# A rank table in place of a table of moves sets the order of a kernel of two long convolutions and two MLPs

## The chip, the cores and the metric

The kernel runs on one core of one Trainium2 chip. The metric is the device time of one execution in microseconds; less is better. The median of three runs of the kernel before is 847.91 us (849.39, 845.15 and 847.91). The execution that was profiled took 850.39 us.

## What is computed

A tensor x of 2048 rows of 640 passes four residual steps, twice a gated long convolution and twice a two-layer MLP with ReLU. Cut to what matters:

```
def _A_ref(q, k, v, shift_k, ssm_k, ssm_D):
    k_shift = sum over t of 4 taps of k, weighted by shift_k      # short causal convolution
    kv = k_shift * v
    y = irfft(rfft(kv, 2S) * rfft(ssm_k, 2S))[:S]                 # causal convolution over 2048 rows, by channel
    y = y + kv * ssm_D
    return q * y

def _B_ref(x, w1, w2):                                            # 640 -> 1728 -> 640
    return maximum(x @ w1, 0) @ w2

x = A_q
x = x + _A_ref(layernorm(x), A_k, A_v, A_shift_k, A_ssm_k, A_ssm_D)
x = x + _B_ref(layernorm(x), B_w1, B_w2)
x = x + _A_ref(layernorm(x), A_k, A_v, A_shift_k, A_ssm_k, A_ssm_D)
x = x + _B_ref(layernorm(x), B_w1, B_w2)
```

## The kernel before

**Tiling.** The rows are cut into 8 chunks of 256 (two tiles of 128 rows each), the channels into 5 tiles of 128. The convolution y is the same in both layers, so it is computed once: for each unit of one or two channel tiles, `transform` makes the spectra of kv and of the filter with small fp32 matmuls (`pg`, `pr` and the transpose `pt`), and `products` multiplies spectra of earlier chunks with filter spectra on VectorE (lines 920 and 925, tiles `pacc` and `pd`), then transforms back with fp32 matmuls (`pq`). Spectra that later chunks need go to DRAM (`A`, `G`) and come back as `Ax` and `Gx`.

**The MLP.** `main` is called 20 times. Each call n runs over seven groups j of the hidden width: `mm1` forms `h{n}_{j}` in PSUM (lines 1449 to 1464), ScalarE makes the fp16 high part `hh`, VectorE the low part `hl` (line 1605), and `mm2` multiplies both with w2 into the banks `o` and `oc` (lines 1433 to 1436). Each fp32 product is three fp16 products of high and low parts. The first two chunks go through the MLP in halves of 128 rows: `mm1` then moves 128 columns, and `mm2` moves 512 and then 128 columns by turns. From chunk 2 on `mm1` moves 256 columns. The calls for chunks 6 and 7 use a Strassen-like form (lines 1384 and 1494). The input of `mm1` is transposed by DMA: four transposes per chunk (line 1318) write `xT{chunk}_{layer}_0{x}`, x = 0 for the high and 1 for the low part, one for each tile of 128 rows. The matmuls of line 1449 with x = 0 need both tiles of part 0.

**fp32 matmuls.** Where a unit has two tiles and comes late enough, `mm3` (lines 577 to 579) makes three matmuls of a rounded fp32 format from the parts of its operands; elsewhere (lines 754, 777, 815, 947, 966) plain fp32 is used, which the trace shows as two records for each matmul.

**What sets the order.** Every operation is recorded in `Plan` with its engine, a cost, what it reads and writes, and a priority. `order` then replays the list in modelled time, and each engine takes the ready operation of the lowest priority for which buffers are free. The result is one fixed instruction stream for each engine, and each engine works through its stream in order; SP's stream issues nearly all DMAs, POOL's the accumulating ones. `best` decides the priorities: operations of class `CRIT` (the start) keep theirs, all others get a key. Before, the keys came from `latest`, which goes backward from the end, repeated four times, and were then pushed about by the table `MOVES`: 693 seeded random nudges of some keys by up to 15 us.

Of the kernel before, what the change touches and what calls it, by code (L numbers as in the profile page):

```python
# [21 lines left out]
P = 128  # L22
S = 2048
# [35 lines left out]
MOVES = ((),) * 4 + (  # L59
# [194 lines left out]
class Plan:  # L254
# [64 lines left out]
    def again(self, kept, key):  # L319
        for o, left, prio in kept[0]:  # L320
            o.left, o.ready, o.start = left, 0.0, None
            if prio[0] != CRIT:
                o.prio = (key[o], o.seq)
# [1513 lines left out]
```

## Time and profile before

| what | before |
| --- | --- |
| runs, us | 849.39, 845.15, 847.91 |
| profiled execution, us | 850.39 |
| its span, first to last instruction, us | 848.6 |
| ScalarE busy | 61% of the span |
| GpSimd busy | 5% of the span |
| HBM traffic over the span | 187 GB/s |

The span is what the rows below cover; 1.8 us of the profiled time lie outside it. Times in a timeline are counted from the span's start. A matmul's start is measured and its length modelled, so its cost in a dense stretch is read from one start to the next.

### The profile page before, as it was taken

The page shows a single profiled execution, that of the slowest core. Times are in us where ns is not written, and L with a number is a line of the kernel's source. Part 1 is how long each engine was busy: PE and PEld are TensorE (multiplying, and loading weights), DVE is VectorE, ACT ScalarE, POOL GpSimd, SP SyncE. Part 2 cuts the span into 40 slices and gives each one's busy share as a digit, 9 for nine tenths or more (in the row PEclk, how much of TensorE's full clock was granted, in tenths as well). Part 3 has the DMA queues.
Part 4 walks back from the last instruction along what each step waited for, and adds up shares of the span by engine and source line. Part 5 has one row for each costly group of instructions (what it writes and reads, how often), then busy time and mean ns, then how long its engine had stood idle before and what let it go on. Part 6 is the DMA issues. An engine that isn't in the chain of part 4 may idle for free.

```text
span 848.6 us, 20004 instructions
## 1 busy us (share of the span) xinstructions
PE 836.8 (99%) x7937; PEld 668.0 (79%) x7937; DVE 778.7 (92%) x1404; ACT 518.3 (61%) x1233; POOL 43.8 (5%) x54
## 2 busy tenths in 40 slices
PE   8999999999998999999999999999999999999998
PEld 6987878888877778777787777777777788888886
DVE  6999999999998899999999999999797799988676
ACT  5798588456784576646657375555515386867531
POOL 0000000000001011011010101010100000000000
PEclk9999999999999999999999999999999999999999
DMA  8995868986989889796997959598977466051200
GB/s 296 394 325 201 266 185 257 313 282 177 314 260 264 277 233 285 233 286 180 226 300 210 260 173 225 164 194 250 247 254 245 115 211 151 22 140 26 58 33 32
DMA packets 138000, 181.68 MB, mean 214 GB/s; under 512 B 53809, under 2 KB 95537, under 8 KB 137906
## 3 DMA queue, kind: packets, MB, share of 16 engines
q1 hardware_dynamic: 129586, 169.91, 65.3%
q0 software_dynamic: 8320, 10.49, 8.3%
q8 instruction: 62, 1.02, 0.5%
q14 instruction: 32, 0.26, 0.1%
HBM read 124.59 MB, written 34.08 MB: 187 GB/s over the span
## 4 chain that ended last, share of the span: by engine, by line
PE 70%; DVE 19%; DMA 4%; ACT 3%; issue 2%; SPq 1%; DVEq 0%; POOLq 0%; ACTq 0%
PE h L1461 8%; PE h L1462 8%; PE h L1464 8%; PE o L1434 6%; PE o L1433 6%; PE o L1384 6%; PE o L1436 6%; PE h L1449 3%; DVE pd L920 3%; DVE pacc L925 3%; PE oc L1433 2%; PE oc L1434 2%; PE pg L754 2%; PE h L1451 1%; PE oc L1436 1%
## 5 line engine op out<-in xcount | busy, mean ns | idle before, releaser
L1461 PE MATMUL h<-xT,w 128*128 128x256 f16 (+1 forms) x1030 | 237.1, 250 | 0.7 <-DVE hl L1610 0.4
L1462 PE MATMUL h<-xT,w 128*128 128x256 f16 (+1 forms) x1030 | 237.0, 250 | 0.0
L1464 PE MATMUL h<-xT,w 128*128 128x256 f16 (+1 forms) x1030 | 237.0, 250 | 0.0
L1433 PE MATMUL o<-w,hh 128*128 128x512 f16 x336 | 127.3, 379 | 0.0
L1434 PE MATMUL o<-w,hh 128*128 128x512 f16 x336 | 127.3, 379 | 0.0
L925 DVE TENSOR_TENSOR pacc<-pacc,pd 128x1536 f32<-128x1536 f32 (+1 forms) x75 | 123.3, 1643 | 0.5
L1462 PEld LDWEIGHTS <-w 128*128 128x128 f16 x1130 | 110.6, 98 | 15.9 <-issue 0.9
L1461 PEld LDWEIGHTS <-w 128*128 128x128 f16 x1130 | 110.5, 98 | 14.7
L1464 PEld LDWEIGHTS <-w 128*128 128x128 f16 x1030 | 100.8, 98 | 6.7
L1604 ACT ACTIVATE hh<-h 128x512 f16<-128x512 f32 (+1 forms) x97 | 46.8, 483 | 71.2 <-PE h L1464 40.3
L1433 PEld LDWEIGHTS <-hh 128*128 128x128 f16 x672 | 65.7, 98 | 29.0
L1434 PEld LDWEIGHTS <-hh 128*128 128x128 f16 x672 | 65.8, 98 | 28.2
L920 DVE TENSOR_TENSOR pd<-Ax,Gx 128x768 f32<-128x768 f32 x83 | 78.1, 949 | 6.7 <-DMA Gx<-G 6.6
L1436 PE MATMUL o<-w,hl 128*128 128x512 f16 x208 | 78.8, 379 | 0.0
L1433 PE MATMUL oc<-w,hh 128*128 128x128 f16 x336 | 73.8, 220 | 0.0
L1434 PE MATMUL oc<-w,hh 128*128 128x128 f16 x336 | 73.6, 219 | 0.0
L1436 PEld LDWEIGHTS <-hl 128*128 128x128 f16 x416 | 40.7, 98 | 25.1 <-DVE hl L1605 0.6
L1449 PE MATMUL h<-xT,w 128*128 128x256 f16 (+1 forms) x400 | 57.4, 251 | 2.2 <-DMA xT<-xh 2.2
L651 ACT ACTIVATE tp<-kt,shs 128x256 f32<-128x256 f32 (+1 forms) x78 | 43.6, 575 | 18.9 <-DVE acc L725 17.2
L1436 PE MATMUL oc<-w,hl 128*128 128x128 f16 x208 | 45.6, 219 | 0.4 <-DVE hl L1605 0.4
L920 DVE TENSOR_TENSOR pd<-at,Gx 128x768 f32<-128x768 f32 x46 | 43.0, 950 | 0.7 <-DMA Gx<-G 0.5
L1449 PEld LDWEIGHTS <-w 128*128 128x128 f16 x400 | 36.3, 98 | 7.8 <-issue 2.5
(276 smaller groups left out, 1974.8 us busy)
## 6 DMA issues: line engine op xcount, KB each, us to landing
Ax<-A SPq DMA_DIRECT2D x89, 384.0 KB, 4.2
Gx<-G SPq DMA_DIRECT2D x89, 384.0 KB, 4.3
G<-gt SPq DMA_DIRECT2D x14, 768.0 KB, 5.0
A<-at SPq DMA_DIRECT2D x14, 768.0 KB, 5.7
ws<-in_w SPq DMA_DIRECT2D x28, 320.0 KB, 6.5
y<-Y SPq DMA_DIRECT2D x22, 320.0 KB, 4.7
x<-in_q SPq DMA_DIRECT2D x16, 320.0 KB, 5.7
gs<-in_hF SPq DMA_DIRECT2D x20, 256.0 KB, 4.7
```

Source lines behind the costliest of these rows:

```text
L651: ACT.activation(o[:, i : i + m], kview(i, m, j), AF.Copy, scale=shs[:, t, j : j + 1])
L920: ew(f"mac{j % POOLMOD}", 768, lambda e, x=dst[i], av=av, gv=gv: e.tensor_mul(x.t, av(), gv()), [ax, gx], [dst[i]], pr_)
L925: dve(768 * (hi - lo), lambda lo=lo, hi=hi, pd=pd: DVE.tensor_add(acc[:, lo:hi], acc[:, lo:hi], pd[:, lo:hi]), [*sums[lo:hi], *dst[lo:hi]] ...
L1384: PE.matmul(b[:, c : c + w], x, y[:, z : z + w], start=done[i] == 1, stop=end, skip_group_check=fin)
L1433: PE.matmul(z, hh[:, c], wh[:, d], start=(j == JS[0] and i == 0 and (h == 0 or s == S[0])), stop=False)
L1434: PE.matmul(z, hh[:, c], wl[:, d], start=False, stop=end and tail)
L1436: PE.matmul(z, hl[:, c], wh[:, d], start=False, stop=end)
L1449: PE.matmul(p[:, z], wh, xv(t, x), start=b and x == 0, stop=e and x == 1)
L1461: PE.matmul(p[:, z], wh, xv(t, 0), start=b, stop=False)
L1462: PE.matmul(p[:, z], wh, xv(t, 1), start=False, stop=tail and e)
L1464: PE.matmul(p[:, z], wl, xv(t, 0), start=False, stop=e)
L1604: act(2 * R, lambda pv_=pv_, hh=hh: ACT.activation(hh.t, pv_(), AF.Relu), [src], [hh], URGENT)
```

## The change

`best` no longer computes keys. It decodes a table `RANKS` with one 16-bit number for each recorded operation and takes that number as the priority; `CRIT` operations keep theirs as before. `latest`, `move`, `again` and `MOVES` are gone. `order`, the recorded operations, their costs, the buffers and everything that is computed are as they were. Both programs have the same instructions on every engine: 7818 matmuls, 1149 activations, 510 DMAs on SP and 40 on POOL. Lines below the table are 124 lower in the changed file (577 becomes 453).

```
-MOVES = ((),) * 4 + (
-    (309216, 1, -282, 918, 30), (849944, 1, -295, 905, 30), (690276, 4, 198, 1398, 30), (179395, 8, 53, 113, 100), (409021, 2, 40, 190, 30), (254445, 4, -151, 249, 30),
...
+RANKS = (
+    "5&#zf000311ONp91^@>D2>=QJ3jhoN4ge1T5C9PX695zd6#y0h7yuan8UPyr9RMBx9{?Z#Apj!)Bmf8iB>*P?0{|QVA^;5lDgY<|D*!A2FaR_FF90(DHvl;RJ^(-fEdVh9H~=;PJOD%hLjXqrO#o2<"
...
     def best(self):
-        ...
-        key = self.latest(*self.order())
-        for move in MOVES:
-            if move:
-                self.move(key, *move)
-            else:
-                key = self.latest(*self.again(kept, key))
-        return self.again(kept, key)
...
+        ranks = np.frombuffer(base64.b85decode(RANKS), "<u2").tolist()
+        for o, r in zip(self.ops, ranks, strict=True):
+            if o.prio[0] != CRIT:
+                o.prio = (r, o.seq)
         return self.order()
```

Three places of the two orders follow.

**TensorE, the first transform of chunk 2** (`pr02_0`, in the call n = 3 of `main`). LDWEIGHTS rows load the weights of the fp16 matmul behind them. Before:

```order
L1462 MATMUL h3_1_2310<-xT0_1_11_2198,w0_11_678 128x128
L1464 LDWEIGHTS w0_11_678
L1464 MATMUL h3_1_2310<-xT0_1_10_2190,w0_11_678 128x128
L577 MATMUL pr02_0_2352<-sh2_0_2264,cMh_1206 128x2x128
L578 MATMUL pr02_0_2352<-sl2_0_2286,cMh_1206 128x2x128
L579 MATMUL pr02_0_2352<-sh2_0_2264,cMl_1722 128x2x128
```

And now:

```order
L1310 MATMUL o20_1929<-w1_51_1317,hh2_5_2223 128x512
L1312 LDWEIGHTS hh2_5_2223
L1312 MATMUL o20_1929<-w1_51_1317,hh2_5_2223 128x512
L453 MATMUL pr02_0_2361<-sh2_0_2201,cMh_1226 128x2x128
L454 MATMUL pr02_0_2361<-sl2_0_2298,cMh_1226 128x2x128
L455 MATMUL pr02_0_2361<-sh2_0_2201,cMl_1804 128x2x128
```

The group stood behind a 128-column matmul of `mm1` and now stands behind a 512-column one of `mm2`. Counted over the two orders, groups of fp32 matmuls other than transposes that stand behind a 128-column 16-bit matmul are 33 before (11 of them of lines 577 to 579) and 19 now (1 of them).

**SP, the transposes for the first call of chunk 2** (`xT2_0_00` and `xT2_0_01`, the high and the low part, read by the matmuls of `h8_0`). `Ax` and `Gx` are spectra, `gs` and `kt` are inputs of later units. Before:

```order
L907 DMA Ax4_0_1_0_4642<-A1_0_103 128x768
L1318 DMA_TRANSPOSE xT2_0_00_4673<-xh2_0_00_4619 128x5x128
L1318 DMA_TRANSPOSE xT2_0_01_4678<-xh2_0_00_4619 128x5x128
L1318 DMA_TRANSPOSE xT2_0_00_4673<-xh2_0_01_4671 128x5x128
L670 DMA gs04_1_4716<-in_hF 128x2x256
L670 DMA gs14_1_4728<-in_hF 128x2x256
L1318 DMA_TRANSPOSE xT2_0_01_4678<-xh2_0_01_4671 128x5x128
L907 DMA Gx4_0_3_0_4760<-G2_0_125 128x768
```

And now:

```order
L783 DMA Ax4_0_1_0_4655<-A1_0_103 128x768
L1194 DMA_TRANSPOSE xT2_0_00_4673<-xh2_0_00_4628 128x5x128
L1194 DMA_TRANSPOSE xT2_0_00_4673<-xh2_0_01_4632 128x5x128
L546 DMA gs04_1_4699<-in_hF 128x2x256
L783 DMA Gx4_0_3_0_4719<-G2_0_125 128x768
L1194 DMA_TRANSPOSE xT2_0_01_4734<-xh2_0_00_4628 128x5x128
L1194 DMA_TRANSPOSE xT2_0_01_4734<-xh2_0_01_4632 128x5x128
```

The second transpose of the high part moved from third to second place; the two of the low part now stand behind one load of `gs` and one of `Gx`. On TensorE the first ten matmuls of `h8_0` keep their place in the sum of matmul work; the first that reads the low part came 5.8 us of matmul work behind them and now comes 3.3 us behind them (ten matmuls of `h8_0`, six of `mm2` and twelve of `pr` stand between).

**VectorE, ahead of the low part of the first hidden group of call 6** (`hh6_0`, line 1605; `h6_2` needs its PSUM bank). Before:

```order
L925 TENSOR_TENSOR pacc3_1_3631<-pacc3_1_3631,pd3_1_2_3678 128x1536
L1676 SCALAR_TENSOR_TENSOR x1_1_1147,sp1_0_1_3830<-oc5_3393,winv_118,x1_1_1147 128x128
L782 TENSOR_TENSOR gt3_3_3879<-pg03_3_3834,ob3_3_3872 128x2x2x128
L1605 SCALAR_TENSOR_TENSOR hh6_0_3877<-h6_0_3764,hh6_0_3877 128x256
L783 TENSOR_TENSOR gt3_3_3879<-pg03_3_3834,ob3_3_3872 128x2x2x128
```

And now:

```order
L1552 SCALAR_TENSOR_TENSOR x1_1_1070,sp1_0_1_3823<-o51_3468,winv_118,x1_1_1070 128x512
L796 TENSOR_TENSOR pd3_1_4_3843<-Ax3_1_2_1_3640,Gx3_1_1_1_3724 128x768
L1552 SCALAR_TENSOR_TENSOR x1_1_1070,sp1_0_1_3823<-oc5_3469,winv_118,x1_1_1070 128x128
L601 TENSOR_TENSOR acc4_0_3769<-acc4_0_3769,tp34_0_3836 128x512
L658 TENSOR_TENSOR gt3_3_3892<-pg03_3_3808,ob3_3_3845 128x2x2x128
L1481 SCALAR_TENSOR_TENSOR hh6_0_3888<-h6_0_3825,hh6_0_3888 128x256
```

Over the whole stream two operations more stand ahead of `hh6_0` than before, the multiply `pd3_1_4` and the tap addition `acc4_0`, which both came behind it. TensorE needs it at the same place of its matmul work.

More of the change, by code (lines that the diff above doesn't have):

```diff
@@ L1 @@
+import base64
 import heapq
@@ L294, in best @@
     def best(self):
-        tiles = list({id(t): t for o in self.ops for t in o.tiles}.values())
-        rings = list({id(t.ring): t.ring for t in tiles if t.ring is not None}.values())
-        kept = [(o, o.left, o.prio) for o in self.ops], [(t, t.left) for t in tiles], [(r, r.free, {k: list(v) for k, v in r.lines.items()}) for r in rings]
-        key = self.latest(*self.order())
-        for move in MOVES:
-            if move:
-                self.move(key, *move)
-            else:
-                key = self.latest(*self.again(kept, key))
@@ L305, in best @@
-        return self.again(kept, key)
-    def move(self, key, seed, by, a, b, part):
-        h = np.arange(len(self.ops), dtype=np.uint32) * np.uint32(2654435761) + np.uint32((seed * 40503 + 12345) % 2**32)
-        for shift, mul in ((16, 2246822519), (13, 3266489917)):
-            h = (h ^ (h >> np.uint32(shift))) * np.uint32(mul)
-        h ^= h >> np.uint32(16)
-        g = h * np.uint32(2654435769)
-        g ^= g >> np.uint32(15)
-        for o, x, y in zip(self.ops, h.tolist(), g.tolist()):
-            if a <= key[o] < b and y % 1000 < part:
-                key[o] += by * (x / 2.0**32 * 2.0 - 1.0)
@@ L319, in again @@
[L319 to L323, printed above, removed]
-        for t, left in kept[1]:
-            t.left = left
-        for r, free, lines in kept[2]:
-            r.free, r.lines = free, {k: list(v) for k, v in lines.items()}
-        return self.order()
-    def latest(self, out, end):
-        users = {}
-        for o in out:
-            for t in o.tiles:
-                users.setdefault(t, []).append(o)
-        left, until = {o: len(o.outs) for o in out}, dict.fromkeys(out, end)
-        before = {o: [(d, (0.0 if o.eng == "PE" else PEOUT) if d.eng == "PE" else 0.08 + (o.eng == "PE") * (RPE * LATE(o) + ROOM.get(d.eng, 0.0))) for d in o.deps] for o in out}
-        spare, had = {}, {}
-        for i, o in enumerate(out):
-            for t in o.new:
-                first = t not in had
-                f = spare.setdefault(t.ring, [(-1.0, j, None) for j in range(t.ring.bufs)])
-                if first:
-                    f.sort(key=lambda x: x[:2])
-                    had[t] = f.pop(0)[2]
-                for u in users.get(had[t], ()):
-                    if u is not o and u not in o.deps:
-                        before[o].append((u, 0.0 if u.eng == o.eng == "PE" else PEOUT if u.eng == "PE" else 0.08))
-                        left[u] += 1
-                if first:
-                    f.append((max(u.ready for u in users[t]), i + len(out), t))
-        unit = lambda o: "DMA" if o.nbytes else o.eng
-        open_, cur, latest = {}, {}, {}
-        for o in out:
-            if not left[o]:
-                open_.setdefault(unit(o), []).append(o)
-        while len(latest) < len(out):
-            t, k = max((min(cur.get(k, end), max(until[o] for o in c)), k) for k, c in open_.items() if c)
-            o = max((o for o in open_[k] if until[o] >= t - 1e-9), key=lambda o: (o.start, o.seq))
-            open_[k].remove(o)
-            cur[k] = t - (o.nbytes / RBW if o.nbytes else o.cost)
-            latest[o] = cur[k] - (1.1 + RLAT if o.nbytes else 0.0)
-            for d, lag in before[o]:
-                until[d] = min(until[d], latest[o] - lag)
-                left[d] -= 1
-                if not left[d]:
-                    open_.setdefault(unit(d), []).append(d)
-        for o in out:
-            if o.cls < -3:
-                latest[o] = o.cls * 1e4
-        return latest
```

62 lines of the change are left out of this document (added), and 115 rows, old and new, of the table MOVES.

## The prediction

> **What bounds the kernel now.** I read the first lines of the page, then the waits of TensorE, then busy time in stretches of the span.
>
> ```profile
> span 848.6 us, 20004 instructions
> PE 836.8 (99%) x7937; PEld 668.0 (79%) x7937; DVE 778.7 (92%) x1404; ACT 518.3 (61%) x1233; POOL 43.8 (5%) x54
> ```
>
> TensorE (PE) is busy for 836.8 of 848.6 us, and the change neither adds nor removes a matmul. So only what lies between the matmuls can go: 11.8 us of idle time, and the slots that are longer than they need be. The waits of TensorE, with the engine waited for, the sum in us, how often, and the longest:
>
> ```profile
> PE h L1449 <- DMA xT<-xh: 2.2, 1, 2.2
> PE spin L1693 <- POOL heps L556: 2.0, 1, 2.0
> PE pr L815 <- ACT sh L810: 1.2, 1, 1.2
> PE pt L801 <- ACT gt L757: 0.7, 1, 0.7
> PE h L1461 <- DVE hl L1610: 0.4, 1, 0.4
> PE oc L1436 <- DVE hl L1605: 0.4, 1, 0.4
> PE o L1384 <- DVE gs L1600: 0.3, 1, 0.3
> PE h L1461 <- DVE hh L1605: 0.2, 1, 0.2
> ```
>
> The second to fourth (3.9 us) are the start; the order of the start is untouched, since its operations are of class CRIT. The other five sum to 3.5 us, and that is all the waiting that a new order can take away. The longest of them is one wait for a DMA transpose.
>
> ```profile
> core 0: us, PE busy (x) PEld busy (x) DVE busy (x) ACT busy (x) POOL busy (x), PEclk, DMA share, GB/s
> 100.00:220.00 120.00, 119.79 (x1394) 98.23 (x1393) 117.20 (x212) 77.62 (x197) 0.00 (x0) 1.00 0.81 256
> 320.00:680.00 360.00, 360.00 (x2983) 274.62 (x2981) 340.17 (x487) 195.93 (x465) 31.77 (x30) 1.00 0.83 226
> ```
>
> From 320 to 680 us TensorE never stands still: nothing can be won there, only lost. From 100 to 220 us VectorE (DVE) is busy for 117.20 of 120 us beside a TensorE at 119.79: two engines are full at once, at full granted clock, and whatever one does later the other must cover.
>
> **The change part by part.** It reorders everything by a few microseconds; I cost the fp32 groups, the transposes, and VectorE's work ahead of TensorE's operands.
>
> *fp32 groups.* Here is one group behind a 512-column matmul, and one behind 128-column ones (start, length):
>
> ```profile
> 299.79 0.38 PE L1436 MATMUL o<-w,hl 128*128 128x512 f16 x1
> 299.82 0.47 PE L577 MATMUL pr<-sh,cMh 128*128 128x256 f32 x1
> 300.12 0.28 PE L578 MATMUL pr<-sl,cMh 128*128 128x256 f32 x1
> 300.24 0.28 PE L579 MATMUL pr<-sh,cMl 128*128 128x256 f32 x1
> ```
>
> ```profile
> 131.47 0.22 PE L1462 MATMUL h<-xT,w 128*128 128x128 f16 x1
> 131.53 0.22 PE L1464 MATMUL h<-xT,w 128*128 128x128 f16 x1
> 131.55 0.36 PE L577 MATMUL pr<-sh,cMh 128*128 128x256 f32 x1
> 131.75 0.28 PE L578 MATMUL pr<-sl,cMh 128*128 128x256 f32 x1
> ```
>
> A matmul of the group takes 0.12 us (300.12 to 300.24), a 128-column one 0.055 us on the mean (131.47 to 131.53). Behind 512 columns, 300.12 - 299.79 = 0.33 us, less the group's own 0.12, leaves 0.21 for the 512 columns, which is 512/128 times the short one's slot: the switch is free. Behind 128 columns, 131.75 - 131.53 = 0.22, less 0.12 and 0.055, leaves 0.045: the switch costs some 0.05 us. Weight loads say why:
>
> ```profile
> L1461 PEld LDWEIGHTS <-w 128*128 128x128 f16 x1130 | 110.5, 98 | 14.7
> L577 PEld LDWEIGHTS pr<-sh,cMh 128*128 128x128 f32 x60 | 11.4, 190 | 1.0
> ```
>
> A load takes 190 ns for these weights and 98 ns for fp16, 92 ns more, too long to hide under one 55 ns slot. The 33 dear entries become 19: 14 x 0.05 = 0.7 us less. Bounds: 0 (if something else holds TensorE there anyway) and 14 x 0.092 = 1.3 us.
>
> [...]
>
> All 33 stand in the stretch of the first two chunks, ahead of the wait for the transpose. So these 0.7 us reach the end only if that wait does not eat them.
>
> *The transposes for `h8_0`.* SP's stream, then the pieces:
>
> ```profile
> 255.31 7.25 SPq L1318 DMA_TRANSPOSE xT<-xh  x3
> 262.62 1.13 SPq L670 DMA_DIRECT2D gs<-in_hF  x2
> 263.80 1.35 SPq L1318 DMA_TRANSPOSE xT<-xh  x1
> 265.24 0.54 SPq L907 DMA_DIRECT2D Gx<-G  x1
> ```
>
> ```profile
> L1318 SPq DMA_TRANSPOSE xT<-xh x1: 1581/1581/1581, 255.3 to 255.3; - x1
> L1318 SPq DMA_TRANSPOSE xT<-xh x2: 2607/2736/2865, 257.0 to 259.7; - x2
> DMA to landing us min/median/max: 6.9/7.0/7.0
> DMA to landing us min/median/max: 4.8/4.8/4.8
> 256.98 0.73 ACT L1290 ACTIVATE xh<-xnB 128x640 f16<-128x640 f32 x1
> 264.48 0.22 PE L1464 MATMUL h<-xT,w 128*128 128x128 f16 x1
> 266.88 0.27 PE L1449 MATMUL h<-xT,w 128*128 128x256 f16 x1 [2.19 <-DMA xT<-xh]
> ```
>
> Each transpose holds SP for 1.35 to 2.9 us. The high part's second one is third, issued at 259.7 and landed 7.0 later (266.7), and TensorE, free since 264.5, starts at 266.88. In the new order it is second: its data are ready at 256.98 + 0.73 = 257.7, SP is free from the first at 256.9, so it goes out at 257.7 and lands at 264.7. The wait all but vanishes: 2.2 us. Late next is the low part. Its two transposes follow at 257.7 + 2.9 = 260.6 plus one `gs` load (0.5) and one `Gx` (0.54), so near 261.7; the last is issued 1.4 to 2.6 later, at 263.1 to 264.3, and lands 4.8 to 7.0 after that: 267.9 to 271.3. TensorE now wants it 3.3 us behind 264.7, at 268.0. Before, the same point of the work would have been reached at 266.88 + 3.3 = 270.2. So the site gives between 2.2 us of gain and 1.1 of loss; I take a landing at 269.3, between the middle (269.6) and what the 4.8 us of the last one before would give (268.5 for an issue at 263.7), **0.9 us of gain**. Because this landing sets the time, the 0.7 us of the fp32 groups ends in the wait ahead of it and counts as nothing.
>
> *VectorE ahead of TensorE.* At the third place of the order, VectorE runs without a pause:
>
> ```profile
> 218.01 0.69 DVE L782 TENSOR_TENSOR gt<-pg,ob 128x512 f32<-128x512 f32 x1
> 218.62 0.41 DVE L1605 SCALAR_TENSOR_TENSOR hh<-h,hh 128x256 f16<-128x256 f32 x1
> 218.95 0.68 DVE L783 TENSOR_TENSOR gt<-pg,ob 128x512 f32<-128x512 f32 x1
> 219.54 0.95 DVE L920 TENSOR_TENSOR pd<-Ax,Gx 128x768 f32<-128x768 f32 x1
> 221.40 0.68 DVE L725 TENSOR_TENSOR acc<-acc,tp 128x512 f32<-128x512 f32 x1
> ```
>
> The last two rows are the operations that now stand ahead of the second, so it ends up to 0.95 + 0.68 = 1.6 us later, and TensorE, which already waits 0.2 us for it, waits up to 1.8. Queued behind it are `h6_2` and all matmuls of call 6. Bounds 0 and 1.6; I take 0.8, half, since VectorE has 2.8 idle us in these 120 to take some of it. But 0.8 - 0.7 for the groups brings TensorE to 264.5 at nearly the old time, and the transposes cover what is left: nothing on the path.
>
> *Behind 268 us.* The wait of `oc` for `hl` (0.4) goes: a group of 30 matmuls of 256 columns now stands between, 30 x half of the 0.21 of a 512-column one, 3.2 us of cover. The waits for L1610 (0.4) and L1600 (0.3) stay, and VectorE's stream ahead of both has grown by more than TensorE's, by the trace's lengths 0.4 us at the one and 1.1 us at the other; bounds 0 and 1.5 together, and I take 0.4, nearer the waits that stand there.
>
> **Sum:** -0.9 (transposes) + 0 (fp32 groups) + 0 (VectorE at 219) - 0.4 + 0.4 = -0.9 us, from 850.39 to 849.5 for the profiled execution. That execution lies 2.5 us above the median of the runs, 847.91, so the forecast for the median is **847.0 us**.
>
> **Rivals.** *All waits go and the groups' saving counts* (faster). For it: the long wait has its cure in the order. Against it: the low part follows close. 3.5 + 0.7 = 4.2 us, so 843.7 (843.1 with the 1.3 us). [...]
>
> *VectorE's queue holds TensorE* (slower). Its place is the stretch from 100 to 260 us, where both engines are full: a held TensorE then delays the PSUM results that VectorE needs, so that VectorE idles too and xh itself, and with it the transposes, comes late. By the order there are three such places (near 132, 219 and 244 us), at 1.6 us each 4.8 us, which makes 852.7. It decides once VectorE's idle time from 100 to 220 us grows from 2.8 to above 7 us. For it: no spare time there; against it: the present order lives with the same load and waits 0.2 us.
>
> *The transpose's wait only moves* to the low part in full: +0.2 for the site and the rest as in the sum, 848.1.
>
> *The change not doing what it says* is excluded by the counts of the order, 33 to 19.
>
> **How the numbers follow.** Runs of the kernel before lie from 845.15 to 849.39, so some 0.5% (4.2 us) is what can be told from no change. Chances: the forecast 0.38, the wait that moves 0.18, the slower rival 0.30, the faster one 0.14. Faster by over 0.5% needs under 843.7, which only the faster rival reaches, and just: 0.14. Slower by over 0.5% is above 852.1, the slower rival: 0.30. Within: 0.56. The range goes from 843.4 (all waits gone) to 853.0 (the slower rival); the forecast's own range is 845.0 to 849.5.
>
> **What would show it.** Right: no wait of `h8_0` for the high part and one of up to 2 us for the low part; fp32 groups behind 512 columns with a free switch; VectorE at 117 us of 120 from 100 to 220; no wait of TensorE from 320 to 680. Wrong: several waits of TensorE for L1605 or L1676 before 260 us, or a wait for a transpose of another chunk. The forecast falls if the sum of TensorE's waits behind the start is under 1 us or over 7 us.

## The result and the profile after

The changed kernel takes **845.40 us** in the median of 22 runs (844.83 to 849.66), the kernel before 848.04 us in 22 runs on the same chip (845.15 to 849.63). The ratio is 0.9972, with a 95% interval of 0.9964 to 0.998: 2.6 us less, 0.3%. That lies inside the range, 843.4 to 853.0. The forecast, 847.0 us, was 1.6 us too high: 2.6 us were gained where 0.9 was worked out. The profiled execution took 845.4 us, 5.0 less than the one profiled before. Of the runs of the experiments below one is left out of its row, a run of the second kernel that took 956.20 us at a granted clock of 0.851.

The page's first line and its line of busy times:

```profile
span 843.6 us, 20032 instructions
PE 833.6 (99%) x7937; PEld 667.3 (79%) x7937; DVE 778.8 (92%) x1404; ACT 518.4 (61%) x1233; POOL 43.8 (5%) x54
```

The waits of TensorE (sum in us, how often, the longest):

```profile
PE spin L1569 <- POOL heps L432: 2.0, 1, 2.0
PE pt L677 <- DVE sd L607: 1.2, 1, 1.2
PE pg L630 <- DVE hf L533: 0.9, 1, 0.9
PE h L1325 <- DMA xT<-xh: 0.8, 2, 0.5
PE pr L691 <- ACT sh L686: 0.7, 1, 0.7
PE h L1337 <- DVE hh L1481: 0.3, 1, 0.3
```

`spin` (matmuls of the identity ahead of the first real ones), `pt`, `pg` and `pr` are the start. Behind it 3.5 us of waiting became 1.1. The wait of 2.2 us for `xT` that stood at 264 us is gone; the 0.8 us for `xT` in this list are two at 473 and 475 us, for the transposes of `h12_0`, where TensorE never waited before. The two stretches that the prediction showed, busy us of each engine:

```profile
core 0: us, PE busy (x) PEld busy (x) DVE busy (x) ACT busy (x) POOL busy (x), PEclk, DMA share, GB/s
100.00:220.00 120.00, 119.61 (x1383) 98.09 (x1381) 118.16 (x213) 76.99 (x203) 1.02 (x1) 1.00 0.84 259
320.00:680.00 360.00, 359.15 (x2980) 274.19 (x2978) 337.94 (x488) 196.94 (x468) 31.70 (x30) 1.00 0.83 226
```

From 100 to 220 us nothing is better (119.61 against 119.79, VectorE at 118.16 against 117.20). From 320 to 680 us 0.85 us are lost.

**A measure for all runs.** Busy time hides slots that are too long, so I use the gaps instead: from one matmul's start to the next one's, less the slot of its form in a dense stretch (55.7 ns for 128 fp16 columns, 109.4 for 256, 215.8 for 512, 119.5 for a matmul of lines 577 to 579). The slots sum to 828.4 us in both kernels. The gaps are summed by position in the matmul work, in us of work, so that orders can be compared:

| gaps, us | start, to 17 | 17 to 205 | 205 to 249 | 249 to 256 | 256 to 300 | 300 to 450 | 450 to 670 | 670 to end |
| --- | --- | --- | --- | --- | --- | --- | --- | --- |
| before | 4.98 | 2.51 | 0.86 | 2.36 | 1.20 | 0.04 | -0.03 | 0.60 |
| after | 3.69 | 2.51 | 0.43 | 0.00 | 0.01 | 0.05 | 1.14 | 0.00 |

A further 1.35 us, at the spin ahead of the first column, are the same in all kernels here. The difference of the table is 4.7 us, which is what the last matmul's end moved (844.46 to 839.76). Of it 3.55 lie between 249 and 300 us of work, where `h8_0` is.

The 1.3 us at the start are no part of the change. There the profile before has a stretch in which TensorE was granted half of its clock (the column PEclk: 1.00 is the full clock), and the one after has none:

```profile
9.49:12.90 3.41, 1.63 (x8) 1.27 (x9) 2.04 (x5) 1.88 (x4) 0.00 (x0) 1.00 1.05 380
12.90:16.31 3.41, 3.41 (x9) 2.70 (x8) 3.00 (x7) 2.49 (x6) 0.00 (x0) 0.50 1.01 352
```

3.41 us at 0.50 are worth 1.7, an estimate from these two figures. The first run below has before's start and no such stretch, and its gaps there are 3.67 us, 1.31 less than before's 4.98 and close to the 3.69 after.

### The profile page after: what moved, and what is told of

The parts are those of the page before. It is cut to its first block, busy times and chain, and to the rows that moved or that the text cites. A ratio compares the mean times of both kernels' runs of the same rounds, so it can differ in the third digit from the quotient of the medians.

```text
span 843.6 us, 20032 instructions
## 1 busy us (share of the span) xinstructions
PE 833.6 (99%) x7937; PEld 667.3 (79%) x7937; DVE 778.8 (92%) x1404; ACT 518.4 (61%) x1233; POOL 43.8 (5%) x54
## 3 DMA queue, kind: packets, MB, share of 16 engines
q8 instruction: 62, 1.02, 0.5%
## 4 chain that ended last, share of the span: by engine, by line
PE 76%; DVE 16%; ACT 3%; issue 2%; DMA 2%; SPq 0%; DVEq 0%; ACTq 0%
PE o L1260 9%; PE h L1337 8%; PE h L1338 8%; PE h L1340 8%; PE o L1310 6%; PE o L1309 6%; PE o L1312 6%; PE h L1325 3%; DVE pd L796 2%; PE h L1327 2%; PE oc L1309 2%; PE oc L1310 2%; DVE pacc L801 2%; PE oc L1312 1%; DVE acc L601 1%
```

## The experiments

Ten of these kernels are one of the two orders with a few operations moved, the eighth is the changed order itself and the eleventh joins the two. In all of them the order is written out as a list and the instructions are the same. Line numbers of these kernels are 138 lower than before's. Each was timed beside the kernel before on one chip, whose median was 847.71 (28 runs, for the first four), 847.93 (35, for the next four) and 847.77 (35, for the last four). One number needs explaining ahead: the share of runs under 846.7 us. All runs of the changed kernel but one lie there, 33 of 34 with the eighth run's. Of the kernel before it is 35 of 120 (2 of the 22 above and 33 of these 98), and its fastest, 844.69, is close to the changed kernel's fastest, 844.42.

| run | median us (range, runs) | ratio, 95% interval | under 846.7 |
| --- | --- | --- | --- |
| 1 transposes | 848.64 (845.24 to 850.62, 12) | 1.0005 (0.9989 to 1.0021) | 2 |
| 2 groups | 851.06 (848.62 to 852.03, 10) | 1.0035 (1.002 to 1.0051) | 0 |
| 3 both | 849.16 (847.62 to 853.03, 12) | 1.0019 (1.0003 to 1.0036) | 0 |
| 4 after, less the new wait | 844.44 (844.19 to 845.19, 5) | 0.9956 (0.9938 to 0.9973) | 5 |
| 5 transposes and `hh` | 847.92 (846.26 to 850.85, 12) | 1.0011 (0.9995 to 1.0027) | 1 |
| 6 `hh` | 848.18 (846.58 to 851.7, 12) | 1.0011 (0.9996 to 1.0026) | 1 |
| 7 after, transposes undone | 844.95 (844.61 to 845.89, 12) | 0.9974 (0.9962 to 0.9987) | 12 |
| 8 after again | 845.49 (844.42 to 846.65, 12) | 0.9977 (0.9964 to 0.9991) | 12 |
| 9 `xh` | 847.90 (844.65 to 848.93, 12) | 1.0000 (0.9984 to 1.0016) | 5 |
| 10 `xh`, transposes and `hh` | 847.64 (845.66 to 850.2, 12) | 1.0003 (0.9988 to 1.0018) | 4 |
| 11 before, then after | 846.23 (845.33 to 850.18, 12) | 0.9991 (0.9977 to 1.0004) | 7 |
| 12 fourth, three more moves | 844.86 (843.6 to 845.62, 12) | 0.9969 (0.9955 to 0.9983) | 12 |

And the gaps of their profiled executions (us, by matmul work):

| run | start, to 17 | 17 to 205 | 205 to 249 | 249 to 256 | 256 to 300 | 300 to 450 | 450 to 670 | 670 to end |
| --- | --- | --- | --- | --- | --- | --- | --- | --- |
| 1 | 3.67 | 2.50 | 0.63 | 0.01 | 2.49 | 0.03 | -0.03 | 0.83 |
| 2 | 3.67 | 4.17 | 1.38 | 0.35 | 4.08 | 0.03 | -0.03 | 0.48 |
| 3 | 3.87 | 4.18 | 1.38 | 0.00 | 4.19 | 0.03 | -0.03 | 0.78 |
| 4 | 4.65 | 2.40 | 0.45 | 0.00 | 0.01 | 0.05 | 0.04 | 0.00 |
| 5 | 4.82 | 2.67 | 0.62 | 0.01 | 2.71 | 0.03 | -0.03 | 0.68 |
| 6 | 3.64 | 2.52 | 0.62 | 4.01 | 0.01 | 0.03 | -0.03 | 0.79 |
| 7 | 4.40 | 2.39 | 0.44 | 0.00 | 0.01 | 0.12 | 0.03 | 0.00 |
| 8 | 3.61 | 2.62 | 0.45 | 0.00 | 0.01 | 0.05 | 0.43 | 0.00 |
| 9 | 3.96 | 2.51 | 0.88 | 0.01 | 0.01 | 0.03 | -0.03 | 0.58 |
| 10 | 3.18 | 2.51 | 1.02 | 0.01 | 2.17 | 1.04 | -0.03 | 0.72 |
| 11 | 4.14 | 2.58 | 2.29 | 0.15 | 0.01 | 0.05 | 0.07 | 0.00 |
| 12 | 4.12 | 2.15 | 0.36 | 0.01 | 0.48 | 0.05 | 0.85 | 0.00 |

In the second run, and by an estimate in the third, the column from 256 to 300 us holds a stretch at half clock, and in the sixth run the one from 249 to 256 us does (last section). The 1.04 us of the tenth run from 300 to 450 us are one wait for VectorE's `hl` at 459 us, which no other run has and nothing here explains.

### First: the transposes alone

```diff
 SP, kernel before
  DMA_TRANSPOSE xT2_0_00 <- xh2_0_00
+ DMA_TRANSPOSE xT2_0_00 <- xh2_0_01
  DMA_TRANSPOSE xT2_0_01 <- xh2_0_00
- DMA_TRANSPOSE xT2_0_00 <- xh2_0_01
  DMA gs04_1, DMA gs14_1
```

> The kernel before with one edit: in SyncE's order the second transpose of the high part of h8_0 goes ahead of the first one of the low part. Theory A (the wait at 264 us was only for the late transpose, and what stands behind it has room): the wait of 2.4 us goes, and the two smaller waits at 278 and 304 us stay, 845.6 us against 848.0. Theory B (my prediction: the low part is late next): of 2.4 us 0.9 go, 847.1 us, with a wait of about 1.5 us on the low part's transpose. Theory C (the wait is set by ScalarE and VectorE, which fill the tiles that are transposed): no change, 848.0 us.

The wait at 264 us went (2.36 to 0.01), no wait for the low part came, and the time stayed. The time is what theory C says, but the wait that it called fixed went; no theory had both. The 2.4 us came back between 256 and 300 us of work, 1.20 to 2.49. The waits of TensorE name ScalarE and VectorE, and ScalarE's timeline (start, length, instruction, idle time ahead and for whom) names the cause:

```profile
PE oc L1295 <- ACT hh L1466: 1.1, 1, 1.1
PE h L1323 <- DVE hl L1472: 0.5, 1, 0.5
PE oc L1298 <- DVE hl L1467: 0.4, 1, 0.4
```

```profile
268.21 0.72 ACT L513 ACTIVATE tp<-kt,shs 128x512 f32<-128x512 f32 x1
274.12 0.63 ACT L534 ACTIVATE hr<-hr 128x512 f32<-128x512 f32 x1 [5.19 <-DMA gs<-hr]
274.65 0.58 ACT L1466 ACTIVATE hh<-h 128x512 f16<-128x512 f32 x1
```

ScalarE stands for 5.19 us at `hr`, and `hh` of `h8_0`, which TensorE needs by way of `oc`, stands behind it. `hr` is multiplied by -1 in place, so it has to wait until POOL's accumulating transfer has added it to `gs`; and that transfer waits for the load of `gs`, which stands on SP behind the transposes. The profile before shows the same chain, on POOL and on ScalarE:

```profile
267.85 0.91 POOL L673 DMA_DIRECT2D gs<-hr  x1 [6.39 <-DMA gs<-in_hF]
272.11 0.72 ACT L651 ACTIVATE tp<-kt,shs 128x512 f32<-128x512 f32 x1
276.73 0.63 ACT L672 ACTIVATE hr<-hr 128x512 f32<-128x512 f32 x1 [3.90 <-DMA gs<-hr]
277.26 0.58 ACT L1604 ACTIVATE hh<-h 128x512 f16<-128x512 f32 x1
```

Here the sum of all gaps up to 300 us of work, 13.25 us, says how late TensorE is; in the first run it is 10.65. `hr` starts at 276.73 and 274.12. The differences are 2.60 and 2.61 us. TensorE's lateness in this stage follows `hr` to 0.01 us, with the wait for the transpose and without it.

### Second and third: the groups of fp32 matmuls

In TensorE's order of the kernel before, 13 operations between 76 and 250 us move by one or two places; two of them:

```diff
 PE, kernel before
+ pr11_2 <- sh1_2, cM
  hb1 <- tb, down
- pr11_2 <- sh1_2, cM
...
- pg03_1, pg13_1 <- gh, gl, cGh, cGl (12 matmuls)
  mm2 of hh5_0 (6 matmuls)
+ pg03_1, pg13_1 <- gh, gl, cGh, cGl (12 matmuls)
```

> The kernel before with TensorE's order alone changed: 12 groups of fp32 matmuls between 76 and 250 us stand one or two places earlier or later, so that they come less often behind 128-column fp16 matmuls (10 such places are left there of 22; the change leaves 11). Theory A (TensorE's time is a plain sum): 12 x 0.05 = 0.6 us less, 847.4 us against 848.0. Theory B (my prediction: the transposes of h8_0 are set by ScalarE, VectorE and SyncE, and the wait for them swallows it): 848.0 us, with the gaps of TensorE 0.6 us shorter until 249 us and the wait at 264 us 0.6 us longer.

> The two edits together, on the kernel before. If the sum of the gaps is plain: the gain of the first run plus 0.6 us (845.0 us where the transposes alone give 845.6). If the wait for h8_0 stays the bound of this stage (my prediction): no better than the transposes alone, 847.1 us.

Neither expectation for the second run came: it is slower by 0.35% (0.2 to 0.51). Each place that went saved its 0.055 us in the trace (13 went, 33 to 20; the expectation counted 12), but the gaps from 17 to 205 us grew from 2.51 to 4.17, by waits that were not there before:

```profile
PE oc L1298 <- DVE hh L1467: 0.7, 2, 0.4
PE h L1323 <- DVE hh L1467: 0.6, 1, 0.6
PE pg L639 <- DVE ys L861: 0.2, 1, 0.2
```

A group that changes places with `mm1` or `mm2` moves the moment at which VectorE must have `hh` ready, or has PSUM to empty, by the length of either (by the slots above 0.8 us for six matmuls of `mm2`, 1.4 for twelve of `pg`), and VectorE had no such slack there: TensorE now waits 0.7 and 0.6 us for `hh`. 13 x 0.055 = 0.7 us are saved, and up to 249 us the gaps are 2.2 us larger all the same. Then the wait for the transpose shrinks to 0.35, as TensorE comes later, and `hr` holds TensorE as before: it starts at 277.43, 3.31 us later than in the first run, and the gaps up to 300 us are 4.35 us larger. The 1.0 us between the two come close to the stretch at half clock behind `hr` (280.1 to 283.5 us, granted clock 0.51), 1.7 us by the estimate above, less the gap of 0.6 at 301 us, which the second run does not have. The third run shows the same with the transposes moved. The rank table moved groups too, with VectorE's and ScalarE's order made to fit; even so the gaps from 17 to 205 us are 2.51 in both kernels. This was one way to move the groups and not the change's own.

### Fifth and sixth: `hh` ahead of `hr`

```diff
 ACT, kernel before (fifth run: with the first run's transposes)
+ ACTIVATE hh8_0 <- h8_0
  ACTIVATE hr4_1 <- hr4_1
- ACTIVATE hh8_0 <- h8_0
```

> The kernel before with the transposes of the first run and, on ScalarE, hh of h8_0 one place earlier, ahead of the multiplication of hr by -1, which waits until a transfer has read hr. Theory A (in the first run the 2.4 us came back as waits of 1.2 and 0.6 us at 274 us, because ScalarE stands at hr for 5.2 us, hh of h8_0 stands behind it, and VectorE's hl and TensorE's oc stand behind hh): both edits together take the wait at 264 us and those at 278 and 304 us, 2.4 + 1.2 = 3.6 us less than before in the gaps, about 844.5 us against 847.9. Theory B (VectorE has no time left in this stage, its queue is the bound): as the first run, no gain, 848 us.

> The kernel before with the move of hh of h8_0 on ScalarE alone. Theory A: the wait of 2.4 us for the transpose stays, the waits at 278 and 304 us (1.2 us together) go or shrink to half: 846.7 to 847.3 us against 847.9. Theory B: no change, 847.9 us.

In the sixth run the waits at 278 and 304 us are gone, as theory A says, and the wait for the transpose stays; the time does not fall. In the fifth run nothing is gained either. ScalarE now does `hh` at once, and stands at `hr` all the same; behind `hr` is now `ob`, which empties the bank that `pt` needs:

```profile
272.47 0.60 ACT L1466 ACTIVATE hh<-h 128x512 f16<-128x512 f32 x1 [2.21 <-PE h L1311]
276.13 0.63 ACT L534 ACTIVATE hr<-hr 128x512 f32<-128x512 f32 x1 [3.06 <-DMA gs<-hr]
PE pt L663 <- ACT ob L643: 1.4, 1, 1.4
```

So in the fifth run theory A was right on each wait and wrong on the time: ScalarE's queue handed the lateness from `hh` on to `ob`, which stood next, and TensorE waited 1.4 us for that. The sixth run is another case. There `hr` starts at 275.64 without idle time ahead of it, and the profiled execution has a stretch at half clock behind the wait for the transpose (last section): its gaps from 249 to 256 us are 4.01 us against 2.36 before, 1.65 more, which is more than the 1.2 us that it saved. Why the median of its 12 runs does not fall isn't shown. Theory B (VectorE is the bound) isn't borne out: in the fifth run VectorE too stands idle for 3.2 us, for a result that ScalarE has behind `hr`.

### Seventh and eighth: the change without the new order of the transposes, and again

```diff
 SP, changed kernel
  DMA_TRANSPOSE xT2_0_00 <- xh2_0_00
+ DMA_TRANSPOSE xT2_0_01 <- xh2_0_00
  DMA_TRANSPOSE xT2_0_00 <- xh2_0_01
  DMA gs04_1, DMA Gx4_0_3_0
- DMA_TRANSPOSE xT2_0_01 <- xh2_0_00
```

> The changed kernel with one part undone: SyncE issues the low part's first transpose of h8_0 ahead of the high part's second one again. Theory A (the order of the transposes is worth the wait of before where ScalarE is out of the way): a wait of 1.5 to 2.4 us stands at 263 us again, 847.2 us against 845.4. Theory C (the new order on ScalarE and VectorE fills the tiles so much earlier that the transposes have slack): 845.4 us.

> The changed kernel again, on this chip, its order written out as a list: 845.4 us by the result, 2.6 us below the kernel before. If the gain belongs to the order and not to a chip, the gaps by stage are those of the first profile within 0.3 us from 17 us on, and few runs show a granted clock below 0.999 (1 of 22 in the result, 13 of 28 of the kernel before here).

The seventh run says theory C: with the old order of the transposes the changed kernel loses nothing (844.95, no gap at 249 to 300 us). The eighth repeats the result on another chip, stage by stage within 0.11 us but for the wait at 474 us, 0.43 in place of 1.14. What it expected of the clock did not come: 4 of its 12 runs have a granted clock below 0.999, and 10 of the 35 of the kernel before. That mean also takes in the end of the span, where TensorE has nothing left to do: in the eighth profile, whose mean is 0.999, the last matmul ends at 839.1 us of 843.0, and the clock is halved from 841.5 us on, which costs nothing. Why the order of the transposes does not matter is in SP's stream and ScalarE's timeline of the changed kernel, and below them of the seventh run:

```profile
253.65 2.68 SPq L1194 DMA_TRANSPOSE xT<-xh  x2
256.38 0.58 SPq L546 DMA_DIRECT2D gs<-in_hF  x1
252.91 1.35 ACT L1166 ACTIVATE xh<-xnB 128x640 f16<-128x640 f32 x2
269.66 0.60 ACT L1480 ACTIVATE hh<-h 128x512 f16<-128x512 f32 x1
271.45 0.63 ACT L548 ACTIVATE hr<-hr 128x512 f32<-128x512 f32 x1 [1.19 <-DMA gs<-hr]
```

```profile
254.25 5.36 SPq L1180 DMA_TRANSPOSE xT<-xh  x3
259.67 0.57 SPq L532 DMA_DIRECT2D gs<-in_hF  x1
271.35 0.63 ACT L534 ACTIVATE hr<-hr 128x512 f32<-128x512 f32 x1 [0.49 <-DMA gs<-hr]
```

Both tiles of `xh` are full at 252.91 + 1.35 = 254.3 us; before, the second was full at 256.98 + 0.73 = 257.7, with `tp`, `hh` and `ob` between the two. The transposes start at 253.65 instead of 255.31, two of them hold SP for 2.68 us where three held it for 7.25, and the first load of `gs` goes out at 256.38 instead of 262.62. `hr` starts at 271.45 instead of 276.73. `hh` of `h8_0` stands ahead of `hr` in the changed order, which is the fifth run's move. In the seventh run three transposes took 5.36 us, the load of `gs` went out at 259.67, and `hr` still started at 271.35.

### Ninth to eleventh: where the gain comes from

```diff
 ACT, kernel before (tenth run: with the fifth run's moves)
  ACTIVATE xnB2_0_00
+ ACTIVATE xnB2_0_01
  ACTIVATE xh2_0_00
+ ACTIVATE xh2_0_01
  ACTIVATE tb
- ACTIVATE xnB2_0_01
  ACTIVATE tp, hh7_6, ob
- ACTIVATE xh2_0_01
```

> The kernel before with ScalarE's and VectorE's order alone changed at one place: the second half's xnB and xh of h8_0 stand right behind the first half's, ahead of tb, tp, hh and ob, on ScalarE, and xh's low parts stand side by side on VectorE. SyncE's and TensorE's orders are those of before. Theory A (what was late is the filling of the tile: ScalarE has it at 257.7 us in the kernel before, at 254.3 in the changed one; the transposes and, behind them on SyncE, the loads that hr waits for come 2 us earlier with it): the gaps of TensorE from 249 to 300 us of its work shrink from 3.6 us to at most 1.2, 845.5 us against 847.9. Theory B (the transfers themselves are the bound here, and start late for another reason): 847.9 us, no gap smaller than 2.4 us in that stage.

> The same, with the transposes of the first run and the order of hh and hr on ScalarE of the fifth. Theory A: nothing is left of the 3.6 us between 249 and 300 us, 844.3 us. Theory B: as the fifth run, a gap of 2.4 us or more, 847.9 us.

> All engines run the order of before up to 235 us of the list's time and the changed order from there. Theory A (the gain belongs to the stage of h8_0): the gaps until 235 us are those of before, those from 249 to 300 us are gone, 844.5 to 845.5 us against 847.9, by how large the new wait at 474 us is in a run. Theory B (the gain comes from the first 235 us, where the groups of fp32 matmuls were moved, and the stage of h8_0 only shows it): 847 us or more.

On VectorE the ninth and tenth run have the two low parts of `xh` side by side too. The ninth run's profiled execution is theory A's: no gap from 249 to 300 us, span 844.0. SP and ScalarE there:

```profile
253.24 1.35 ACT L1152 ACTIVATE xh<-xnB 128x640 f16<-128x640 f32 x2
254.06 5.49 SPq L1180 DMA_TRANSPOSE xT<-xh  x3
259.60 1.41 SPq L532 DMA_DIRECT2D gs<-in_hF  x2
272.13 0.63 ACT L534 ACTIVATE hr<-hr 128x512 f32<-128x512 f32 x1 [1.53 <-DMA gs<-hr]
```

But its median is that of the kernel before: 5 runs lie from 844.65 to 846.69 and 7 from 847.74 to 848.93, and the profile shows one of the five. The tenth run, with more moves, was caught on the other side, and its median is theory B's too:

```profile
274.20 0.63 ACT L534 ACTIVATE hr<-hr 128x512 f32<-128x512 f32 x1 [2.53 <-DMA gs<-hr]
PE pt L663 <- ACT ob L643: 2.0, 1, 2.0
```

Its load of `gs` went out at 259.93, 0.3 us later than in the ninth, and `hr` started 2.1 us later: the transfers between took longer, 14.3 us against 12.5. TensorE's lateness follows `hr` here too. Fifth and tenth run have the same ScalarE order from `hh` of `h8_0` on; `hr` starts 1.93 us apart (276.13 and 274.20), and the gaps up to 300 us of work differ by 1.93 (12.17 and 10.24). From the ninth run's 272.13 the first run's numbers (274.12 and 10.65) would allow a lateness of 8.66 without a wait, and TensorE had 8.72: it just missed waiting.

The eleventh run takes the changed order from 235 us of the list on. From 249 us on its gaps are those after, less most of the wait at 474 us; 7 of its 12 runs are under 846.7 us, and the new waits at the seam (2.29 us from 205 to 249, 0.86 before) cost 1.4 us. So by the gaps the gain lies behind 235 us, and theory B, that the first 235 us bring it, is not borne out. The times alone would not say it: 846.23 lies between what the two theories forecast, and the interval of its ratio, 0.9977 to 1.0004, includes 1.

### Fourth and twelfth: can the changed kernel be bettered

```diff
 SP, changed kernel
  DMA_TRANSPOSE xT4_0_00 <- xh4_0_00
+ DMA_TRANSPOSE xT4_0_00 <- xh4_0_01
  DMA Gx6_0_1_0
  DMA_TRANSPOSE xT4_0_01 <- xh4_0_00
- DMA_TRANSPOSE xT4_0_00 <- xh4_0_01
- DMA Gx6_0_0_0
  DMA_TRANSPOSE xT4_0_01 <- xh4_0_01
+ DMA Gx6_0_0_0
```

> The changed kernel with one edit: in SyncE's order the second transpose of the high part of h12_0 goes ahead of a load of Gx and of the low part, and the last load of Gx there goes behind the low part's second transpose. Theory A (the new wait of 1.1 us at 474 us, the only one of that size left, comes from the loads ahead of the transposes, which wait for their buffer): it goes, 844.3 us against 845.4. Theory B (the tiles are filled too late by VectorE, or the loads of Gx now come late and VectorE with them): no change, 845.4, or up to 846.5.

> The fourth run's kernel (the changed one without the wait at 474 us) with three more moves of one or two places, for the three largest waits left behind the start (0.5 us at 102, 0.2 at 188, 0.3 at 232 us, each for VectorE's hh, which empties the buffer that TensorE writes next): hh goes ahead of a sum or a gl on VectorE, twice, and ahead of at on ScalarE, once. Theory A (each is a wait for one late instruction): 1.0 us less than the fourth run's 844.4, so 843.4 us. Theory B (as with the groups of the second run, an instruction moved up there sends another wait down the queue): 844.4 us or more.

SP's stream of the changed kernel shows what stands among the transposes of `h12_0`: a load of `Gx` that keeps SP for 1.88 us. Behind it, the stream of the fourth run:

```profile
463.01 1.21 SPq L1194 DMA_TRANSPOSE xT<-xh  x1
464.27 1.88 SPq L783 DMA_DIRECT2D Gx<-G  x1
466.25 3.72 SPq L1194 DMA_TRANSPOSE xT<-xh  x2
470.03 1.45 SPq L783 DMA_DIRECT2D Gx<-G  x1
471.57 1.35 SPq L1194 DMA_TRANSPOSE xT<-xh  x1
```

```profile
463.89 3.09 SPq L1180 DMA_TRANSPOSE xT<-xh  x2
467.07 0.53 SPq L769 DMA_DIRECT2D Gx<-G  x1
467.70 3.51 SPq L1180 DMA_TRANSPOSE xT<-xh  x2
```

The wait is gone and the median is 844.44, as theory A says, with five runs within 1.0 us. But the seventh and eighth run have the changed kernel's order at this place, the same load keeps SP for 0.56 and 0.57 us there, and the gaps are 0.03 and 0.43: the wait comes and goes without the edit. That the edit took it away isn't shown. The twelfth run took 0.3 us out of the gaps up to 249 us (2.85 to 2.51), and got back 0.48 from 256 to 300 and 0.85 at 581 us, for a `hl` of VectorE, at a place that no move touched. By its time it is theory B; that the moves caused the wait at 581 us isn't shown. Both have a median below the changed kernel's 845.40 and 845.49, but the intervals overlap and the fourth has five runs. That it beats the change is likely, and not shown.

## Why the prediction was right where it was, and where it was wrong

The forecast missed by 1.6 us of 847, and its gain stood in the wrong term: the 0.9 us came from a trade of one transpose's wait for another's that did not happen, and what was gained came by way of `hr`, which it does not mention. That the number came so near is largely luck.

- **fp32 groups, costed at 0.** The price was right, 0.050 to 0.056 us at each such place in the trace, and so was that none of it reaches the end: 2.51 us of gaps from 17 to 205 us in both kernels (a gap of 0.5 for `hh` at 102 us is new in the changed one). The reason was not. It is not the wait for the transpose that swallows the saving; a moved group lays new waits for VectorE's `hh` around it (second run).
- **The transposes, -0.9 with bounds -2.2 to +1.1.** This step failed. "Late next is the low part" is what no profile shows: nowhere is there a gap of 0.1 us for the low part of `h8_0`. The step took TensorE's wait for the transpose as the bound of the stage. Taken away alone it is worth nothing (first run), and put back in the changed kernel it costs nothing (seventh). The bound was `hr`, whose transfers start in the same queue of SP and which came 12 us later (276.7, against 264.5 us). The prediction quoted the load of `gs` in that queue as an obstacle in front of the low part, and never asked who waits for `gs`.
- **Behind 268 us, -0.4 + 0.4.** Mis-sized, for the same reason. The waits at 278 and 304 us were read as small ones with causes of their own. They were the rest of the lateness that `hr` set, 1.20 us in gaps, and they went together. The wait for L1600, which the step kept, went as well: 0.60 us of gaps behind 670 us before and 0.00 after. It is in every run that has the order of before there (0.48 to 0.83 us), and what took it away isn't shown.
- **VectorE at 219 us, 0.** Right as a sum, not in its terms: the 0.8 us of new waiting, which the groups and the transposes were to cover, never came. The gaps from 205 to 249 us fell from 0.86 to 0.43. VectorE idles 1.84 us from 100 to 220, and the slower rival needed 7.
- **"From 320 to 680 us nothing can be won, only lost."** Right, and it was lost: 1.14 us at `h12_0` in the first profile, 0.43 in the eighth run. The text named such a wait for another chunk's transpose as a sign against it; it is a loss that no term held. The sum of the waits behind the start, 1.1 us, is just above the 1 us under which the forecast was to fall.
- **"The order of the start is untouched."** True of TensorE alone. SP's, ScalarE's and VectorE's orders at the start did change. It cost and gave nothing that the runs show: 3.18 to 4.98 us over all profiles, with either start.
- **The basis.** The sum was made on an execution at 850.39 us, with a stretch at half clock and the full wait. The runs from 845.15 up were on the table, and the spread was used only as noise. It was the larger part of the story: the order before also reaches 844.69 us, in some runs, and the changed one stays under 846.7 nearly always. The clock is not all of that: the runs with a granted clock of 1.000 have a median of 847.37 us before (38 of 98) and of 845.46 changed (24 of 34), 1.9 us less. The range's lower end, called "all waits gone", is 843.4, where the rival's own sums give 843.7 and 843.1.

What made the gain, then: the new order fills `xh` 3.4 us earlier on ScalarE and sends the load of `gs` 6.2 us earlier, so that `hr` comes 5.3 us earlier and the transfers may take longer without holding TensorE. Of each of these three numbers 1.7 us are not that order's: TensorE itself is 1.7 us ahead at 249 us of work in the profile after (gaps of 6.63 against 8.35 us), 1.3 of it by the start. Shown is that TensorE's lateness follows `hr` (two pairs of runs, 0.01 us or less apart), that the gaps which went lie behind 235 us (eleventh), and that the order of the transposes does not bring it (first, seventh). The groups do not either, as far as the gaps from 17 to 205 us and the eleventh run say. That an early `hr` makes the gain is argued: the ninth run has it in its profile and not in its median. That the spread of the kernel before is the spread of these transfers is argued, from one profiled execution of each kernel. Not tried: the load of `gs` moved ahead of the transposes alone, which would be the direct test.

## What to carry to other kernels

The waits of TensorE in this stage were not a list to be added up; they were readings of one lateness. Before a wait is priced, look on every engine in the stage for idle time behind an instruction in the queue (here ScalarE, 3.9 us at `hr`, though no wait of TensorE named it) and follow it to the place in SP's stream where its transfer is issued. And where the runs of a kernel spread by 5 us, a profile is one draw of them: a better order may hardly lower the best time, but give the slow transfers room.

## What was not expected of the hardware

**In the sixth run a wait of 2.3 us left a gap of 4.01.** Behind the first 5 us and ahead of the end, TensorE was busy for less than half of a stretch of 3.41 us five times in these profiles: 1.63 us before (9.49 to 12.90 us), 1.66 after (8.80 to 12.21), 1.34 in the second run (276.7 to 280.1), 1.13 in the sixth and 1.57 in the tenth. After three of them, before and in the second and sixth run, the next 3.41 us ran at a granted clock of 0.50 to 0.51, after the other two at 1.00. The third run has a sixth such place by an estimate: its gaps from 256 to 300 us are 4.19 us against 2.49 in the first run, and the mean granted clock of its profile is 0.997 against 1.000. Below are the sixth run's, with the kernel before's wait for the transpose in it; the same wait in the profile before; and the tenth run's:

```profile
262.42:265.83 3.41, 1.13 (x17) 0.94 (x15) 3.41 (x7) 0.38 (x1) 0.00 (x0) 1.00 1.00 240
265.83:269.24 3.41, 3.41 (x18) 3.10 (x16) 0.86 (x3) 0.60 (x1) 0.91 (x1) 0.50 1.09 363
```

```profile
262.08:265.49 3.41, 2.62 (x29) 1.73 (x26) 3.41 (x5) 0.98 (x2) 0.00 (x0) 1.00 1.27 164
265.49:268.90 3.41, 2.02 (x18) 1.95 (x19) 2.81 (x7) 0.02 (x1) 0.91 (x1) 1.00 1.15 339
268.90:272.31 3.41, 3.41 (x30) 2.54 (x29) 2.17 (x4) 3.41 (x7) 0.41 (x1) 1.00 1.06 381
```

```profile
287.12:290.53 3.41, 1.57 (x14) 1.47 (x15) 3.41 (x5) 3.31 (x11) 0.00 (x0) 1.00 1.04 383
290.53:293.94 3.41, 3.41 (x30) 2.16 (x28) 3.41 (x6) 2.56 (x11) 0.86 (x1) 1.00 0.87 320
```

The stretches are laid on the times at which the granted clock changes: in the trace before it falls to 0.50 at 12.90 us, is back at 1.00 at 16.32 and falls again at 849.17, behind the span, and the 832.85 us at 1.00 are 244 times the 3.413 us at 0.50. In the sixth run the wait falls into one of them (busy 1.13 of 3.41) and the next one runs at 0.50: that is why its gap at 249 to 256 us is 4.01. In the profile before the wait of 2.2 us for the same transpose lies across two (2.62 and 2.02), the next one runs at 1.00, and the gap is 2.36. Busy time alone doesn't divide the cases: behind 1.63 us busy at the start of the kernel before the clock was halved, behind 1.57 in the tenth run it was not. The granted clock over a whole run was 0.997 or less in 22 of 98 runs of the kernel before and in 1 of 34 of the changed one; below 0.999 it was in 42 and in 5.

**Two transfers in a row vary by 3.4 us.** From the issue of the load of `gs` to the start of `hr`, with POOL's accumulating transfer between, it took 11.7 us in the seventh run (259.67 to 271.35), 12.5 in the ninth (259.60 to 272.13), 13.6 in the eighth, 14.1 in the profile before and 15.1 in the fifth run and after (256.38 to 271.45). The DMA share of the stretches from 262 to 272 us before, shown above, is 1.06 to 1.27.
